# Turning the states' exponentials on TensorE instead of through DRAM, and VectorE's sums of the last batch placed later

## The chip, the cores and the metric

The kernel runs on one core of one Trainium2 chip. The metric is the device time of one execution in microseconds (us). Six executions of the kernel before gave a median of 720.07 us, from 718.45 to 720.99.

## The reference

`x` is (8, 8, 512, 64): 8 batches, 8 heads, 512 tokens of 64 values. `state` is (8, 8, 32, 64): 32 state tokens for each batch and head. Everything is float32.

```python
scores  = scale * x @ state^T;   a  = softmax(scores);   xread = a @ state     # 512 tokens
scores2 = scale * state @ x^T;   a2 = softmax(scores2);  sread = a2 @ x        # 32 state tokens
y = concat([xread, sread], axis=2) -> (8*544, 512)       # heads side by side
h = y @ w_in                                             # 512 -> 2048
out = (h * sigmoid(1.702 * h)) @ w_out                   # 2048 -> 512
```

## The kernel before

**How the work is cut.** Batch 0 and the up-projection of batch 1 run first, while the weights are still being rounded. Then comes one pass for each of the batches 1 to 7: `strassen_two(key, ...)` makes the down-projection of batch `key` as a Strassen product of seven partial products P1 to P7. In the passes 2 to 7, P5, P6, P3, P7 and P4 are themselves made as Strassen products of seven small products (`strassen_low`, matmuls in L693), so that P6.3 means "within P6, behind its third small product". Pass 1 (called *plain* in the code) does so for P6 and P7 alone. While pass `b` runs, the attention of batch `b + 1` is worked in at hooks such as "P5.6" or "P6", and the up-projection of a batch (`up_strassen`, L1091) runs at the head of its pass. After pass 7 the 256 state tokens of all batches ("sr") go through `up_strassen("sr", ...)` and `strassen("sr", ...)`, and the kernel ends with their four stores.

**What sets the order.** The order is written out by hand: each engine takes its instructions strictly in the order of the code, and a hook puts its work into the queues of all engines at that place. `hooks_next(b)` lists what is worked in for batch `b`. SyncE issues all DMAs, in order.

**The states' softmax.** `att_scores` leaves the scores of the 32 states of 4 heads in 128 partitions, one bank of 128x512 for each half `g` (0 or 1). `att_s_exp` makes the exponentials (`e2`, ScalarE, L372) and their sums, and `s_norm` the inverse of the sums (VectorE, two tiny operations for each half, L378 and L379). `att_sread` (TensorE, L500) needs the exponentials turned, tokens on the partitions, in the tile `eT`. For batches 0 and 1 `att_eT` does it (L489): four 128x128 transposes on TensorE for each half, and a ScalarE copy out of PSUM (L490). For batches 2 to 7 the turn goes through memory: `eT_out` writes the blocks to the DRAM tile `squares` in four DMAs (L468), `eT_in` fetches them back in four more (L476), and `eT_turn` finishes within 32x32 blocks by one VectorE transpose for each half (L480). The inverse sums are then applied to the small result of `att_sread` by two ScalarE operations (L509).

**The sums of a pass.** Each Strassen product needs sums of its operands, made by VectorE (`tt`, L751; on the weights `T_of`, L1235). `low_load` fetches sums of the weights that are kept in DRAM: `low_load(6, 1)` is issued behind P5 and read by P3's second small product, `low_load(3, 0)` is issued behind P6 and read by P7's second. P7's left operand S3 has four steps of sums, `steps3`, of two 128x256 additions each. They stand behind P3 and behind the hook "run". In the passes 2 to 6 that hook holds TensorE work (`att_sread`, `att_M`); in pass 7, which has no next batch, it holds only the issue of one load.

**The sums for the state tokens.** `sr_sums` lists 20 VectorE operations: 0 to 15 on halves of `w_in` (128x512 each, L1051), 16 to 19 on the state tokens (128x256). They are worked into pass 7, as are five operations `low_third` that put quarters of `w_out` back as they were (L1235).

**`strassen_low` and the banks.** Of its seven small products, the first and third write bank x, the second, fifth and seventh bank y, the fourth and sixth bank z. ScalarE copies x after the first product (L702) and after the third (L708), VectorE adds after the others (L698), and a product that writes a bank again waits until it was read. `up_strassen` works in the same way with `begin(u)`, `end(u - 1)` and `middle(u)` for u = 0 to 3; its additions are L1101, and `s12` and `s3` make sums for the product that follows.

Of the kernel before, what the change touches and what calls it, by code (L numbers as in the profile page):

```python
# [20 lines left out]
def kernel(  # L21
# [337 lines left out]
            nc.vector.tensor_scalar(mx, mx, scale, None, ALU.mult)  # L359
            a["mx2"].append(mx)  # L360

    e2_room = {}

    def att_s_exp(b, room=None):
        a = A[b]
        if room is None:
            room = e2_room[b] = apool.tile([P, NPR, S], FP32, tag="xT", name=f"e2_{b}")
        a["e2"] = []
        for g in range(NG):
            e = room[:, g]  # L370
            sm = apool.tile([P, 1], FP32, tag="sm2", name=f"sm2_{b}_{g}", bufs=4)
            nc.scalar.activation(out=e, in_=a["s"][g], func=AF.Exp, bias=a["mx2"][g], scale=scale, accum_out=sm)  # L372
            a["e2"].append((e, sm))

    def s_norm(b, g):

        e, sm = A[b]["e2"][g]
        nc.vector.tensor_scalar(sm, sm, eps, None, ALU.add)  # L378
        nc.vector.reciprocal(out=sm, in_=sm)  # L379
        if b < 2:  # L380
            nc.vector.tensor_scalar(e, e, sm, None, ALU.mult)

    def att_s_norm(b):
        for g in range(NG):
# [74 lines left out]
        for g in range(NG):  # L459
            nc.scalar.copy(m[:, g], ps[g])  # L460


    squares = dram.tile([Ns, NG * NB, NPR, Ns], FP32, name="squares")

    def eT_out(b):
        for j in range(NPR):
            src = e2_room[b][Ns * j : Ns * (j + 1), :NG].rearrange("n g (t a) -> n (g t) a", a=Ns)
            nc.sync.dma_start(squares[:, :, j], src)  # L468

    def eT_in(b):  # L470

        a = A[b]
        a["eT"] = apool.tile([P, NG, SCH, P], FP32, tag="eT", name=f"eT_{b}")
        v = squares.rearrange("n (k i) j a -> i n k (j a)", i=SCH)
        for i in range(SCH):
            nc.sync.dma_start(a["eT"][Ns * i : Ns * (i + 1)].rearrange("n g c q -> n (g c) q"), v[i])  # L476

    def eT_turn(b, g):
        t = A[b]["eT"][:, g].rearrange("p c q -> p (c q)")
        nc.vector.transpose(t, t)  # L480

    def att_eT(b, g):

        a = A[b]
# [7 lines left out]
    def att_sread(b):  # L492

        a = A[b]
        ps = att_ps([P, NG, D], f"sr_{b}")
        for g in range(NG):
            for c in range(SCH):
                for j in range(NPR):
                    st = slice(Ns * j, Ns * (j + 1))
                    nc.tensor.matmul(  # L500
                        ps[st, g], a["eT"][:, g, c, st], xn[b][:, c, NG * j + g],
                        start=(c == 0), stop=(c == SCH - 1),
                    )
        sr = apool.tile([P, P], FP32, tag="sr", name=f"sr_{b}")
        if b < 2:
            nc.scalar.copy(sr, ps.rearrange("p g d -> p (g d)"))
        else:
            for g in range(NG):
                nc.scalar.activation(out=sr[:, D * g : D * (g + 1)], in_=ps[:, g], func=AF.Copy, scale=a["e2"][g][1])  # L509
        A[b]["sr"] = sr  # L510

    def att_srT(b):
# [210 lines left out]
    def strassen_two(key, dst, hooks, a4):  # L723
# [10 lines left out]
        def hook(name):  # L734
            for fn, args in hooks.get(name, ()):
                fn(*args)
# [75 lines left out]
        if plain:  # L812
            for fn in first:
                fn()
            p5 = bank(0)
            product(p5, [S1[:, f, :half] for f in range(HF)], T1, "P5")
            hook("P5")
            banks = [h0, h1, o]
        else:

            def at(i):
                for fn in first[i - 1 : i]:
                    fn()
                hook(f"P5.{i}")

            b11, t3, b21, b22 = halves_of(T1)
            strassen_low(left_of(S1, *r), (b11, t3, b21, b22, *low_b), [h0, h1, o], p5, at)
            low_load(6, 1)
            hook("P5")
            o, h0, h1 = low_banks()  # L830
            banks = [h0, o, h1]

# [45 lines left out]
        if plain:  # L878
            for fn in steps3:
                fn()  # L880
            hook("P6")
            p3 = bank(3)
            product(p3, A_of(0, 1), B22, "P3")
            o, h0, h1 = low_banks()
            lowly("P7", left3, T3, low_b, [h0, h1, o], k3, {})
        else:
            hook("P6")
            p3 = o01
            o, h0, h1 = low_banks()
            lowly("P3", left12, B22, low_b, [h0, h1, o], p3, {1: steps12[2:3], 2: steps12[3:]})  # L890
            if key + 1 < B:
                low_load(5, 1)
            hook("run")
            for fn in steps3:
                fn()
            hook("T")
            o, h0, h1 = low_banks()
            lowly("P7", left3, T3, low_a, [o, h0, h1], k3, {k + 1: steps4[k : k + 1] for k in range(4)})
            if key + 1 < B:
                low_load(2, 0)  # L900
# [25 lines left out]
    def hooks_next(b):  # L926

        h = {}

        def at(name, fn, *args):  # L930
            h.setdefault(name, []).append((fn, args))

        at("P1a", att_state, b)
        at("P2a", att_scores, b)

        at("P2a", load_x, b)
        at("P2a", att_M, b, 0)
        at("P2a", att_M, b, 1, True)
        at("P2a", att_blocks, b)
        at("P2a", att_s_max, b)  # L940
        at("P2a", att_s_exp, b)
        at("P2a", eT_out, b)
        at("P2a", x_max, b, 0)
        at("P2a", x_sub, b, 0)
        if b > 2:
            at("P5.1", x_exp, b, 0)
            at("P5.6", att_s_norm, b)
            at("P5.6", x_max, b, 1)
            at("P5.7", x_sub, b, 1)
            at("P6.1", x_exp, b, 1)  # L950
        else:
            at("P2a", x_max, b, 1)
            at("P2a", x_sub, b, 1)
            at("P2a", x_exp, b)
            at("P2", att_s_norm, b)
        steps = up_sums(b)

        A[b]["sums"] = {0: steps[9:11], 1: [steps[11], steps[14]]}
        attention = [
            ("P6.1", x_sum, 0), ("P6.3", x_sum, 1), ("P6.3", x_inverse), ("P6.4", x_scale, 0),  # L960
        ]
        if b > 2:
            attention += [("P6.6", x_scale, 1), ("P3.3", x_back, 0), ("P3.4", x_back, 1), ("P3.5", eT_turn, 0), ("P3.6", eT_turn, 1)]
            names = {"T": range(5), "P7.5": (5, 6), "P7.6": (7,), "P4.1": (8,), "P4.5": (12, 13)}
            run, turned = "run", "P7.2"
        else:
            attention += [("P6.5", x_scale, 1), ("P6.6", x_back, 0), ("P6", x_back, 1), ("P6", eT_turn, 0), ("P6", eT_turn, 1)]
            names = {"P3a": range(7), "P7.1": (7,), "P7.2": (8,), "P7.3": (12, 13)}
            run, turned = "P3a", "P3b"
        attention += [("P5", eT_in), (run, att_sread), (run, att_M, 3, True), (run, att_M, 2)]  # L970
        for name, fn, *args in attention:
            at(name, fn, b, *args)
        for name, n in names.items():
            for i in n:
                at(name, steps[i][0], *steps[i][1])
        at(turned, att_srT, b)
        return h
# [92 lines left out]

        return steps, left, [each(v) for v in (r11, r21, r22, *ts)]

    def up_strassen(b, ntok, left, right, between=()):

        QT = ntok // 2
        b11, b21, b22, t1, t2, t3, t4 = right
        banks = {}
# [22 lines left out]
        def add(ps, x, dst):  # L1100
            nc.vector.tensor_tensor(out=dst, in0=ps, in1=x, op=ALU.add)  # L1101


        def begin(u):
            l11, l12, l21, l22, m1, m2, m4 = left(u)
# [2 lines left out]
            c21, _ = quarters(b, NU + u, ntok)  # L1108
            nc.scalar.copy(c21, product(u, "x", l11, b11, True))
            add(product(u, "y", m2, t2, True), c21, c12)  # L1110

        def middle(u):
            l11, l12, l21, l22, m1, m2, m4 = left(u)
# [4 lines left out]
            add(product(u, "y", l21, t3, False), c21, c22)  # L1118
            add(z, c22, c22)
            gelu(c22, c22)  # L1120

        def end(u):
            l11, l12, l21, l22, m1, m2, m4 = left(u)
# [3 lines left out]
            gelu(c21, c21)  # L1127
            add(product(u, "z", m4, b22, False), c12, c12)
            gelu(c12, c12)
            if u:  # L1130
                s12(b, u - 1, ntok)

# [141 lines left out]
    for b in range(1, B):  # L1274
# [18 lines left out]
        else:  # L1293

            steps, left, right = sr_sums()
            order = (
                ("P5.6", 2), ("P6.1", 3), ("P6.2", 6), ("P6.3", 7), ("P6.4", 8), ("P3.3", 9), ("P3.4", 10), ("P3.5", 11),
                ("P7.5", 12), ("P7.6", 13), ("P4.1", 16, 17), ("P4.5", 18, 19), ("P4.6", 14), ("P4.7", 15),
            )
            hooks = {name: [steps[i] for i in n] for name, *n in order}  # L1300
            hooks["P3.6"] = [(low_third, (T1,))]
            hooks["P4.7"] += [(low_third, (t,)) for t in (T2, T3, T4, B22)]
            ahead["P1a"][:0] = [steps[i] for i in (0, 1, 4, 5)]
        for name, first in ahead.items():
            hooks[name] = first + hooks.get(name, [])
# [9 lines left out]
    nb = P // Ns  # L1315
    strassen(
        "sr", B * Ns, lambda r, n: out_s[nb * r.start : nb * r.stop, :, n],
        [[(up_strassen("sr", B * Ns, left, right), ())]],
    )


# [28 lines left out]
```

## Time and profile before

| What | Before |
|---|---|
| median of 6 executions | 720.07 us |
| the profiled execution | 719.47 us, span 717.7 us |
| outside the span | 1.8 us |
| TensorE busy | 700.6 us, 98% of the span |
| VectorE busy | 591.4 us, 82% |
| ScalarE busy | 229.8 us, 32% |
| DMA | 74.73 MB, 135849 packets, 113008 of them under 512 B |

In the lists of instructions a line gives the start in us from the start of the span, the duration (for a merged group: first start to last end), engine, source line, operation, tiles (out<-in) and count, and in brackets how long the engine stood idle before and what it was waiting for. TensorE's matmuls are pipelined: the duration of one is longer than the distance between two starts, so the distance of starts is what a matmul costs in a row. A float32 matmul leaves two records, a transpose leaves one.

### The profile page before, as it was taken

To read this page: it belongs to the slowest core of one execution; us is meant where nothing else is said; L and a number is where in the kernel's file an instruction comes from. 1 tells how busy PE (TensorE), PEld (TensorE's weight loads), DVE (VectorE), ACT (ScalarE), POOL (GpSimd) and SP (SyncE) were. 2 spreads that over 40 slices of the span, in tenths; PEclk is the share of its full clock that TensorE was granted. 3 is DMA by queue.
4 is the path that set the end of the run, shared out by engine and by line. 5 is a ranking of instruction groups with operands and counts; after the bars stand their busy time and mean duration, and the time that the engine had idled before them with its cause. 6 is when DMAs were issued, how large, how long until landed. Compare 5 with 4: busy or idle time off the path is not lost.

```text
span 717.7 us, 12333 instructions
## 1 busy us (share of the span) xinstructions
PE 700.6 (98%) x4903; PEld 557.2 (78%) x4903; DVE 591.4 (82%) x1211; ACT 229.8 (32%) x449; POOL 0.8 (0%) x8
## 2 busy tenths in 40 slices
PE   8989999999899999999999999999999999999996
PEld 3433444467698799888998899879987998899995
DVE  6998899739967999789968997799789986989440
ACT  5686511023114322433233322441243125200210
POOL 0000000000000000000000000000000000000000
PEclk9999999999999999999999999999999999999999
DMA  9921246017344194407450564136432740031001
GB/s 233 359 89 55 92 148 149 2 59 165 93 164 83 34 179 157 92 1 161 150 145 5 108 196 131 26 74 176 160 52 49 172 162 16 1 121 56 16 1 30
DMA packets 135849, 74.73 MB, mean 104 GB/s; under 512 B 113008, under 2 KB 126832, under 8 KB 135792
## 3 DMA queue, kind: packets, MB, share of 16 engines
q1 hardware_dynamic: 135792, 73.94, 38.6%
q8 instruction: 39, 0.64, 0.4%
q14 instruction: 18, 0.15, 0.1%
HBM read 57.93 MB, written 15.99 MB: 103 GB/s over the span
## 4 chain that ended last, share of the span: by engine, by line
PE 85%; DVE 7%; DMA 4%; ACT 2%; issue 1%; SPq 0%; DVEq 0%; ACTq 0%
PE o L1091 17%; PE low L693 17%; PE o L744 13%; PE o L693 8%; PE o L542 7%; PE h L524 7%; PE upx L1091 6%; PE M L320 4%; PE o L585 2%; DVE later L751 1%; PE o L320 1%; PE sr L500 1%; DMA low<-low 1%; PE warm L125 1%; DVE g L751 1%; DMA out_dram<-osb_sr 1%
## 5 line engine op out<-in xcount | busy, mean ns | idle before, releaser
L1101 DVE TENSOR_TENSOR g<-o,g 128x512 f32<-128x512 f32 (+1 forms) x140 | 88.0, 650 | 55.5 <-PE o L1091 54.5
L744 PE MATMUL o<-w_out,g 128*128 128x256 f32 x480 | 107.9, 381 | 0.0
L744 PEld LDWEIGHTS o<-w_out,g 128*128 128x128 f32 x480 | 90.1, 190 | 18.4 <-issue 6.3
L1098 ACT ACTIVATE g<-g 128x512 f32<-128x512 f32 (+1 forms) x84 | 49.8, 600 | 101.9 <-DVE g L1101 101.9
L1091 PE MATMUL upx<-aT,M 128*128 128x256 f32 x192 | 49.3, 379 | 0.0
L1091 PE MATMUL o<-ta,M 128*128 128x256 f32 x192 | 49.3, 379 | 0.0
L1091 PE MATMUL o<-ta,ms 128*128 128x256 f32 x192 | 48.3, 379 | 0.0
L460 ACT COPY M<-M 128x512 f32<-128x512 f32 x64 | 33.2, 596 | 28.1 <-PE M L320 28.1
L1091 PEld LDWEIGHTS o<-ta,ms 128*128 128x128 f32 x192 | 36.5, 190 | 5.0
L1091 PEld LDWEIGHTS o<-ta,M 128*128 128x128 f32 x192 | 36.5, 190 | 5.0
L693 PE MATMUL low<-low,g 128*128 128x128 f32 x304 | 40.2, 275 | 0.0
L1091 PEld LDWEIGHTS upx<-aT,M 128*128 128x128 f32 x192 | 36.1, 190 | 4.7
L693 PEld LDWEIGHTS low<-low,g 128*128 128x128 f32 x304 | 37.0, 192 | 0.0
L693 PE MATMUL low<-sums,later 128*128 128x128 f32 x264 | 35.0, 275 | 0.1
L693 PEld LDWEIGHTS low<-sums,later 128*128 128x128 f32 x264 | 32.7, 192 | 0.7 <-DVE pu L698 0.3
L565 DVE TENSOR_TENSOR later<-g,g 128x512 f32<-128x512 f32 (+1 forms) x32 | 20.8, 650 | 15.0 <-ACT g L527 15.0
L320 PE MATMUL M<-w_in,stT 64*32 64x512 f32 x512 | 32.7, 594 | 0.2 <-ACT eT L490 0.2
L524 PE MATMUL h<-low,M 128*128 128x512 f32 x64 | 29.8, 600 | 1.5 <-DVE low L408 1.5
L524 PE MATMUL h<-aT,M 128*128 128x512 f32 x64 | 28.7, 599 | 1.4 <-ACT M L460 1.4
L542 PE MATMUL o<-w_out,g 128*128 128x512 f32 x64 | 28.7, 594 | 0.0
L693 PE MATMUL low<-w_out,g 128*128 128x128 f32 x216 | 28.5, 275 | 0.0
L542 PE MATMUL o<-w_out,sums 128*128 128x512 f32 x64 | 28.4, 594 | 0.0
(215 smaller groups left out, 1271.5 us busy)
## 6 DMA issues: line engine op xcount, KB each, us to landing
low<-low SPq DMA_DIRECT2D x34, 768.0 KB
later<-in_moe_w_out_dram SPq DMA_DIRECT2D x16, 512.0 KB
xn<-in_x_dram SPq DMA_DIRECT2D x28, 256.0 KB
w_out<-in_moe_w_in_dram SPq DMA_DIRECT2D x12, 512.0 KB
xsq<-in_x_dram SPq DMA_DIRECT2D x96, 64.0 KB
out_dram<-osb SPq DMA_DIRECT2D x18, 256.0 KB
out_dram<-later SPq DMA_DIRECT2D x14, 256.0 KB
squares<-e SPq DMA_DIRECT2D x24, 128.0 KB
```

What stands on the lines that cost most here:

```text
L320: nc.tensor.matmul(ps[g][st], A[b]["stT"][rows, st], rhs(rows, j), start=True, stop=True)
L460: nc.scalar.copy(m[:, g], ps[g])
L524: nc.tensor.matmul(hps, lhs[i], rhs[i], start=(i == 0), stop=(i == n - 1))
L542: nc.tensor.matmul(ops, G[key, f // 2][:, f % 2, P * r : P * (r + 1)], w_out[:, f], start=(f == 0), stop=(f == NF - 1))
L565: nc.vector.tensor_tensor(out=s1, in0=a21, in1=a22, op=ALU.add)
L585: nc.tensor.matmul(ps[:, r], lhs[f][:, P * r : P * (r + 1)], rhs[:, f], start=(first and r == 0 and f == 0), stop=(f == HF - 1), skip_grou ...
L693: nc.tensor.matmul(ps, lhs[f], rhs[:, f], start=(first and f == 0), stop=(f == QF - 1), skip_group_check=True)
L744: nc.tensor.matmul(ps[:, r], lhs[f][:, P * r : P * (r + 1)], rhs[:, f], start=(r == 0 and f == 0), stop=(f == HF - 1), skip_group_check=True,)
L751: nc.vector.tensor_tensor(out=out, in0=x0, in1=x1, op=op)
L1091: nc.tensor.matmul(ps[:, k], lhs[i][:, o : o + P], rhs[i], start=(first and k == 0 and i == 0), stop=(i == n - 1), skip_group_check=True,)
L1098: nc.scalar.activation(out=dst, in_=src, func=AF.Gelu_apprx_sigmoid)
L1101: nc.vector.tensor_tensor(out=dst, in0=ps, in1=x, op=ALU.add)
```

## The change

It does three things.

1. For batches 2 to 7, `eT_out`, `eT_in`, `eT_turn` and the DRAM tile are gone. `s_norm` now scales the exponentials themselves, on ScalarE, at its old place, and `att_eT` (four transposes on TensorE and one ScalarE copy for each half) stands in the hook "P6", between P6 and P3. One plain ScalarE copy takes `att_sread`'s result. In the passes 2 to 6 `x_scale(1)`, `x_back(0)` and `x_back(1)` stand one hook later or in the places that `eT_turn` left.
2. In pass 7 the four steps of `steps3` stand behind P3's third to sixth small product, not behind P3.
3. In pass 7 ten of VectorE's operations for the state tokens (`sr_sums` 10 to 15 and four `low_third`) stand in `up_strassen("sr", ...)`, one behind the additions of each `begin`, `middle` and `end` (there ahead of `s12`), until they are used up; `aside()` places them. `sr_sums` 6 to 9 and one `low_third` move to later hooks.

```diff
     def s_norm(b, g):
...
         if b < 2:
             nc.vector.tensor_scalar(e, e, sm, None, ALU.mult)
+        else:
+            nc.scalar.activation(out=e, in_=e, func=AF.Copy, scale=sm)
-    squares = dram.tile([Ns, NG * NB, NPR, Ns], FP32, name="squares")
-    def eT_out(b):
...
-    def eT_in(b):
...
-    def eT_turn(b, g):
...
     def att_sread(b):
...
-        if b < 2:
-            nc.scalar.copy(sr, ps.rearrange("p g d -> p (g d)"))
-        else:
-            for g in range(NG):
-                nc.scalar.activation(out=sr[:, D * g : D * (g + 1)], in_=ps[:, g], func=AF.Copy, scale=a["e2"][g][1])
+        nc.scalar.copy(sr, ps.rearrange("p g d -> p (g d)"))
...
-            lowly("P3", left12, B22, low_b, [h0, h1, o], p3, {1: steps12[2:3], 2: steps12[3:]})
+            own3 = {1: steps12[2:3], 2: steps12[3:]}
+            if key + 1 == B:
+                own3.update({i + 3: steps3[i : i + 1] for i in range(4)})
+            lowly("P3", left12, B22, low_b, [h0, h1, o], p3, own3)
...
             hook("run")
-            for fn in steps3:
-                fn()
+            if key + 1 < B:
+                for fn in steps3:
+                    fn()
...
-            ("P6.1", x_sum, 0), ("P6.3", x_sum, 1), ("P6.3", x_inverse), ("P6.4", x_scale, 0),
+            ("P6.1", x_sum, 0), ("P6.3", x_sum, 1), ("P6.3", x_inverse), ("P6.4", x_scale, 0), ("P6", att_eT, 0), ("P6", att_eT, 1),
         if b > 2:
-            attention += [("P6.6", x_scale, 1), ("P3.3", x_back, 0), ("P3.4", x_back, 1), ("P3.5", eT_turn, 0), ("P3.6", eT_turn, 1)]
+            attention += [("P3.3", x_scale, 1), ("P3.4", x_back, 0), ("P3.5", x_back, 1)]
         else:
-            attention += [("P6.5", x_scale, 1), ("P6.6", x_back, 0), ("P6", x_back, 1), ("P6", eT_turn, 0), ("P6", eT_turn, 1)]
+            attention += [("P6.5", x_scale, 1), ("P6.6", x_back, 0), ("P6", x_back, 1)]
...
-    def up_strassen(b, ntok, left, right, between=()):
+    def up_strassen(b, ntok, left, right, between=(), beside=()):
...
+        def aside():
+            if beside:
+                fn, args = beside.pop(0)
+                fn(*args)
...
-                ("P5.6", 2), ("P6.1", 3), ("P6.2", 6), ("P6.3", 7), ("P6.4", 8), ("P3.3", 9), ("P3.4", 10), ("P3.5", 11),
-                ("P7.5", 12), ("P7.6", 13), ("P4.1", 16, 17), ("P4.5", 18, 19), ("P4.6", 14), ("P4.7", 15),
+                ("P5.6", 2), ("P6.1", 3), ("P6.3", 6), ("P6.4", 7), ("P7.5", 8), ("P7.6", 9), ("P4.1", 16, 17), ("P4.5", 18, 19),
-            hooks["P3.6"] = [(low_third, (T1,))]
-            hooks["P4.7"] += [(low_third, (t,)) for t in (T2, T3, T4, B22)]
+            hooks["P3.7"] = [(low_third, (T1,))]
+            beside = steps[10:16] + [(low_third, (t,)) for t in (T2, T3, T4, B22)]
```

More of the change, by code (lines that the diff above doesn't have):

```diff
@@ L360, in att_s_max @@
             a["mx2"].append(mx)
-    e2_room = {}
     def att_s_exp(b, room=None):
@@ L366, in att_s_exp @@
         if room is None:
-            room = e2_room[b] = apool.tile([P, NPR, S], FP32, tag="xT", name=f"e2_{b}")
+            room = apool.tile([P, NPR, S], FP32, tag="xT", name=f"e2_{b}")
         a["e2"] = []
@@ L460, in att_M @@
             nc.scalar.copy(m[:, g], ps[g])
-    squares = dram.tile([Ns, NG * NB, NPR, Ns], FP32, name="squares")
-    def eT_out(b):
-        for j in range(NPR):
-            src = e2_room[b][Ns * j : Ns * (j + 1), :NG].rearrange("n g (t a) -> n (g t) a", a=Ns)
-            nc.sync.dma_start(squares[:, :, j], src)
-    def eT_in(b):
[L472 to L476, printed above, removed]
-    def eT_turn(b, g):
-        t = A[b]["eT"][:, g].rearrange("p c q -> p (c q)")
-        nc.vector.transpose(t, t)
     def att_eT(b, g):
@@ L816, in strassen_two @@
             product(p5, [S1[:, f, :half] for f in range(HF)], T1, "P5")
-            hook("P5")
             banks = [h0, h1, o]
@@ L828, in strassen_two @@
             low_load(6, 1)
-            hook("P5")
             o, h0, h1 = low_banks()
@@ L941, in hooks_next @@
         at("P2a", att_s_exp, b)
-        at("P2a", eT_out, b)
         at("P2a", x_max, b, 0)
@@ L966, in hooks_next @@
         else:
-            attention += [("P6.5", x_scale, 1), ("P6.6", x_back, 0), ("P6", x_back, 1), ("P6", eT_turn, 0), ("P6", eT_turn, 1)]
+            attention += [("P6.5", x_scale, 1), ("P6.6", x_back, 0), ("P6", x_back, 1)]
             names = {"P3a": range(7), "P7.1": (7,), "P7.2": (8,), "P7.3": (12, 13)}
             run, turned = "P3a", "P3b"
-        attention += [("P5", eT_in), (run, att_sread), (run, att_M, 3, True), (run, att_M, 2)]
+        attention += [(run, att_sread), (run, att_M, 3, True), (run, att_M, 2)]
         for name, fn, *args in attention:
@@ L1071, in sr_sums @@
         return steps, left, [each(v) for v in (r11, r21, r22, *ts)]
-    def up_strassen(b, ntok, left, right, between=()):
+    def up_strassen(b, ntok, left, right, between=(), beside=()):
+        beside = list(beside)
         QT = ntok // 2
@@ L1110, in begin @@
             add(product(u, "y", m2, t2, True), c21, c12)
+            aside()
         def middle(u):
@@ L1120, in middle @@
             gelu(c22, c22)
+            aside()
         def end(u):
@@ L1129, in end @@
             gelu(c12, c12)
+            aside()
             if u:
@@ L1317 @@
         "sr", B * Ns, lambda r, n: out_s[nb * r.start : nb * r.stop, :, n],
-        [[(up_strassen("sr", B * Ns, left, right), ())]],
+        [[(up_strassen("sr", B * Ns, left, right, beside=beside), ())]],
     )
```

## The prediction

> **What bounds the kernel now.** I read the page first: busy times and the chain that ended last.
>
> ```profile
> PE 700.6 (98%) x4903; PEld 557.2 (78%) x4903; DVE 591.4 (82%) x1211; ACT 229.8 (32%) x449; POOL 0.8 (0%) x8
> PE 85%; DVE 7%; DMA 4%; ACT 2%; issue 1%; SPq 0%; DVEq 0%; ACTq 0%
> ```
>
> TensorE is busy for 98% of the span and carries 85% of the chain. So an instruction added to TensorE costs its full slot, one taken from VectorE, ScalarE or a DMA gains nothing by itself, and the only gain to be had is a wait of TensorE that goes away. The second view is therefore the list of TensorE's waits, the third its instructions in order of time around each of them.
>
> ```profile
> PE sr L500 <- DVE eT L480: 2.3, 1, 2.3
> PE o L1091 <- DVE g L1101: 0.8, 1, 0.8
> PE low L693 <- DMA low<-low: 0.7, 1, 0.7
> PE low L693 <- ACT pu L702: 0.5, 1, 0.5
> PE low L693 <- DVE later L698: 0.2, 1, 0.2
> ```
>
> These are all the waits that the change comes near; the rest lie in the first 95 us or are tails of these. They must be priced by distances of starts, since the idle time is counted from a modelled end.
>
> **Added: the transposes.** Twelve halves of four, 48 in all. Batch 0 already turns its exponentials in this way:
>
> ```profile
> 81.34 1.04 PE L489 MATMUL eT<-ident,e 128*128 128x128 f32 x8
> 82.62 1.58 PE L320 MATMUL M<-w_in,stT 64*32 64x512 f32 x16 [0.24 <-ACT eT L490]
> ```
>
> Eight take 1.04 with the last one's 0.27, so seven distances fill 0.77: 0.11 each, 0.88 for a batch, 48 x 0.11 = **5.28 us**. The pause after these eight (0.24 idle) is the next matmul's wait for a PSUM buffer that the copy must empty. In the new place P3 follows, in other banks, so I take no pause; if it stays, six times 0.24 + 0.17 (the usual overlap of a start with the end before it) = 2.5 us more. That is the upper bound, 7.7; the lower is 5.28, since no row shows a shorter distance.
>
> The Trainium skill speaks against the change here: "TensorE: Matmul & The Clock Gate", Part 4: PE-mode transpose, gives about 275 ns for a transpose in a kernel and says that transposes do not count as activity for the clock. By that figure 48 would cost an estimated 13.2 us and the kernel would lose about 7 us. The trace has the same 272 ns as duration of one, but starts 0.11 apart, and the page's row of granted clock shows 9 in every slice, those with batch 0's and 1's turns included; so I reckon with the distance.
>
> The copies of the turned halves on ScalarE (12 x 0.59, L490's mean) and the scalings (12 x 0.63, L1098's mean on 128x512 in SBUF) add 15 us to an engine that is 32% busy. What is queued behind them matters. The scalings come at P5.6; behind them stands P6's copy of bank x, and P6's third product waits for that.
>
> ```profile
> 562.41 0.16 DVE L379 RECIPROCAL sm<-sm 128x1 f32<-128x1 f32 x1
> 563.60 0.27 ACT L702 COPY pu<-low 128x128 f32<-128x128 f32 x1 [4.25 <-PE low L693]
> 564.25 1.06 PE L693 MATMUL low<-sums,later 128*128 128x128 f32 x8
> ```
>
> The first reciprocal ends at 562.32, two scalings end by 563.6, the copy keeps its 563.60, and it has 0.38 to spare before 564.25. ScalarE sat idle for 4.25 ahead of it: cost nothing. The copies run beside P3's first product (0.89), whose own copy of x comes after it: nothing. `att_sread` reads `eT` a whole P3 later.
>
> **Removed: DMAs and VectorE's turns.** 48 DMAs of 128 KB, and 12 transposes of 0.69 (8.2 us, L480). Both lie beside TensorE, except where TensorE waits for them:
>
> - Pass 1. P3's first half has sixteen records of 0.216 from 185.60, 3.45, and 0.10 for the change of tile, as in pass 6 (574.34 + 0.89 + 0.10 = 575.33). The next matmul could start at 189.15.
>
> ```profile
> 190.84 1.26 DVE L480 STREAM_TRANSPOSE eT<-eT 128x512 f32<-128x512 f32 x2
> 191.56 1.25 PE L500 MATMUL sr<-xn,eT 128*32 128x64 f32 x64 [2.34 <-DVE eT L480]
> ```
>
>   It starts 2.41 late, and its 64 records take 1.18 to the next group, against 1.03 in pass 6: 2.56 in all. In the changed kernel `eT` comes from TensorE and ScalarE ahead of P3, so the whole 2.56 goes. VectorE is next in line: its queue ends with `x_back(1)` at 190.9, while `att_sread`, pushed back by the 0.88, would run from 190.0 to 191.1; the sums behind it overwrite what it reads, so they start with it, 1.6 earlier than now, and no product waits for them before P7. **-2.56.**
> - Pass 2. P3's second product waits for `low_load(6, 1)`:
>
> ```profile
> 265.03 1.06 PE L693 MATMUL low<-w_out,g 128*128 128x128 f32 x8
> 266.82 1.13 PE L693 MATMUL low<-low,spare_M 128*128 128x128 f32 x8 [0.74 <-DMA low<-low]
> 272.35 1.43 PE L500 MATMUL sr<-xn,eT 128*32 128x64 f32 x64
> ```
>
>   1.79 between the starts instead of 0.89, and 0.97 instead of 0.89 for the product itself: 0.98. The transposes stand ahead of P3, so the product asks 0.88 later for a load that is issued as before, and `eT_in`'s four DMAs no longer run beside it: **-0.98**. `att_sread` takes 1.36 to the next group instead of 1.03, as its second half waits for the second turn: **-0.33**.
> - Pass 6: 568.76 to 569.80, then 0.97, the same load: **-0.23**. Passes 3 to 5 show no such wait, so their transposes are a plain loss.
>
> VectorE loses two operations per pass between P6.6 and P3.6, and gets none; `x_back(1)` still ends ahead of the sums that read its result.
>
> **Moved: `steps3` and the ten operations in pass 7.**
>
> ```profile
> 647.85 1.06 PE L693 MATMUL o<-w_out,g 128*128 128x128 f32 x8
> 649.45 1.13 PE L693 MATMUL low<-low,later 128*128 128x128 f32 x8 [0.54 <-ACT pu L702]
> 652.20 1.06 PE L693 MATMUL low<-w_out,g 128*128 128x128 f32 x8
> 653.49 1.16 PE L693 MATMUL low<-w_out,later 128*128 128x128 f32 x8 [0.23 <-DVE later L698]
> 664.31 1.06 PE L1091 MATMUL upx_sr<-srT,w_in 128*128 128x128 f32 x8
> 666.12 1.16 PE L1091 MATMUL o<-ta_sr,w_in 128*128 128x128 f32 x8 [0.75 <-DVE g L1101]
> ```
>
> P7's second product starts 1.60 after the first, not 0.89, and then takes 0.97: 0.79. It needs S3's second step, which VectorE makes at 648.93 (the copy named in the brackets had no part in it). Its sixth waits for an addition in the same backlog: 1.29 and 0.99, so 0.50. In `up_strassen` the third product on bank y waits for an addition that stands behind two L1051 and four L1235: 1.81 and 0.99, so 1.02. Sum 2.31.
>
> In P3 the four steps (0.67 a pair) take the places of three L1051 and one L1235 (0.60 each), so P3's last additions come up to 0.3 later. P3's sixth product already waits 0.05 for one; I book 0.1. In `up_strassen("sr")` one u has five additions, two sums of `s12` (0.42 each) and now three operations of 0.68: 2.9 + 2.0 = 4.9, against seven products of 0.89 = 6.2 on TensorE. The least slack is in `middle`: the addition on y ends 0.42 after it may start, and bank y is asked for again 1.5 after that. So no new wait: **-2.31 + 0.1 = -2.2.** The operations stand ahead of the `begin`, `middle` or `end` that reads them.
>
> **The sum.** 5.28 - 2.56 - 0.98 - 0.33 - 0.23 - 2.2 = **-1.0 us**. The profiled execution goes from 719.47 to 718.4 (span 716.7). It lies 0.6 below the median of the six, so the median goes from 720.07 to 719.0. The bound of what a measurement of this kernel can tell is 0.2%, 1.4 us: 718.6 to 721.5 is "no change".
>
> **Rivals.**
>
> - *The forecast as it stands, 719.0 (0.56).*
> - *The waits move on (0.20).* VectorE is 97% busy from 160 to 192 (31.07 of 32 us) and stays so in P3 of pass 7. If P7 still waits there, 1.3 of the 2.31 is not gained, and if P7 of pass 1 meets VectorE's backlog, up to 0.9 of the 2.56: -1.0 + 1.3 + 0.9 = +1.2, 721.3, or half of that. Against it: VectorE is idle for 2.52 ahead of P7's second addition at 200.34, and pass 7's 3.0 us of sums leave the place where they were waited for.
> - *Slower: the scalings hold up P6's copy of x (0.07).* ScalarE is strictly in order. From the point where the reciprocals come over 0.4 late, or a scaling takes over 0.8 (the dearest 128x512 row of ScalarE is 0.72, L219), P6's third product waits; with one scaling exposed in the passes 2 to 6, 5 x 0.63 = 3.2: -1.0 + 3.2 = +2.2, 722.2. The times at 562 speak against it.
> - *More than forecast (0.17).* Two more waits in pass 1 (its P6, 182 to 184, 0.39 and 0.45 by starts) are VectorE's backlog, and passes 3 to 6 have a late addition of 0.07 each in P3. If the lighter VectorE takes these too: -1.0 - 0.84 - 0.28 = -2.1, 717.9. Nothing that stands ahead of P6 in pass 1 is taken from VectorE, which speaks against the larger part.
> - *The turn was not needed as assumed* cannot be: the order of TensorE's queue shows exactly twelve more groups of four transposes and no other difference.
>
> **The numbers.** The sum of -1.0 lies only 0.4 from the bound of "faster", and the terms are read to 0.1 each, some twelve of them; so of the forecast's own 0.56 I give 0.14 to faster. Faster 0.14 + 0.16 = 0.30; slower 0.07, and 0.01 of the moved waits: 0.08; same 0.62. The range goes from the lighter-VectorE case with some spread, 717.6, to the middle of the moved waits, 720.8.
>
> **What would show it.** Right: 64 L489-like transposes in all (16 before), the new ones in six groups of eight with starts 0.11 apart and P3's first product 0.11 after the last; `att_sread` 0.10 after P3 in every pass, pass 1 included; the wait for `low` gone; in pass 7 no gap over 0.1 from P3 to the state tokens' P1; TensorE's busy time up by about 5, its idle time down by about 6. Wrong: a gap of TensorE on either side of the transposes, ScalarE's L702 later than P6's first product, or the pass from 329 to 405 longer by anything but 0.9.

## The result and the profile after

| | before | after |
|---|---|---|
| median | 720.29 us (718.42 to 722.07, 50 executions) | 718.10 us (717.99 to 718.38, 23 executions) |
| profiled execution | 719.47 us, span 717.7 | 718.08 us, span 716.3 |

The ratio of the times is 0.9973, 95% interval 0.9966 to 0.998: faster by 0.27%. The profiled executions differ by 1.4 us, the medians by 2.2, and the executions of the changed kernel lie within 0.4 us of each other where those of the kernel before ranged over 3.7. The second and third of these were not forecast.

The page's busy times and chain, and of the list of TensorE's waits the two longest rows and the only one behind 100 us:

```profile
PE 703.1 (98%) x4951; PEld 560.8 (78%) x4951; DVE 586.8 (82%) x1199; ACT 241.7 (34%) x467; POOL 0.8 (0%) x8
PE 90%; DVE 3%; DMA 3%; ACT 2%; issue 0%; SPq 0%; DVEq 0%; ACTq 0%
...
PE h L500 <- DVE low L408: 1.5, 1, 1.5
PE h L500 <- ACT M L460: 1.4, 2, 0.8
PE o L669 <- DVE later L674: 0.2, 1, 0.2
```

TensorE's share of the chain rose from 85% to 90%, VectorE's fell from 7% to 3%. The waits of `att_sread` for `eT`, of P3 for the load of `low` and of `up_strassen` for VectorE's additions are no longer in the list; its longest are those of the first 95 us. TensorE's instructions in order of time at the places of the prediction (L469 is the transpose, L480 `att_sread`, L669 the small products, L720 P3 of pass 1, L1071 `up_strassen`):

```profile
185.60 1.04 PE L469 MATMUL eT<-ident,e 128*128 128x128 f32 x8
186.47 3.62 PE L720 MATMUL o<-w_out,g 128*128 128x256 f32 x16
190.02 1.10 PE L480 MATMUL sr<-xn,eT 128*32 128x64 f32 x64
...
569.11 1.04 PE L469 MATMUL eT<-ident,e 128*128 128x128 f32 x8
569.98 1.06 PE L669 MATMUL low<-w_out,g 128*128 128x128 f32 x8
...
648.81 1.06 PE L669 MATMUL o<-w_out,g 128*128 128x128 f32 x8
649.71 1.06 PE L669 MATMUL low<-low,later 128*128 128x128 f32 x8
652.39 1.06 PE L669 MATMUL low<-w_out,g 128*128 128x128 f32 x8
653.28 1.06 PE L669 MATMUL low<-w_out,later 128*128 128x128 f32 x8
664.00 1.06 PE L1071 MATMUL upx_sr<-srT,w_in 128*128 128x128 f32 x8
664.89 1.06 PE L1071 MATMUL o<-ta_sr,w_in 128*128 128x128 f32 x8
```

The eight transposes of a batch take 0.87 from their start to P3's in pass 1 and in pass 6; there is no gap on either side. In the part of pass 7 shown here all distances of products are 0.89 or 0.90. All terms of the forecast stand side by side further down.

### The profile page after: what moved, and what is told of

It reads as the page before. It is cut to its first block, busy times and chain, and to the rows that moved or that the text cites. A ratio compares the mean times of both kernels' runs of the same rounds, so it can differ in the third digit from the quotient of the medians.

```text
span 716.3 us, 12331 instructions
## 1 busy us (share of the span) xinstructions
PE 703.1 (98%) x4951; PEld 560.8 (78%) x4951; DVE 586.8 (82%) x1199; ACT 241.7 (34%) x467; POOL 0.8 (0%) x8
## 4 chain that ended last, share of the span: by engine, by line
PE 90%; DVE 3%; DMA 3%; ACT 2%; issue 0%; SPq 0%; DVEq 0%; ACTq 0%
PE low L669 19%; PE o L1071 17%; PE o L720 14%; PE o L669 9%; PE o L518 7%; PE h L500 7%; PE upx L1071 6%; PE M L320 4%; PE o L561 2%; PE o L320 1%; PE sr L480 1%; PE warm L125 1%; PE upx_sr L1071 1%; DMA out_dram<-osb_sr 1%; PE eT L469 1%; DMA out_dram<-osb 1%
## 5 line engine op out<-in xcount | busy, mean ns | idle before, releaser
L720 PE MATMUL o<-w_out,g 128*128 128x256 f32 x480 | 107.9, 381 | 0.0
L720 PEld LDWEIGHTS o<-w_out,g 128*128 128x128 f32 x480 | 90.1, 190 | 18.4 <-issue 6.3
L1071 PE MATMUL upx<-aT,M 128*128 128x256 f32 x192 | 49.3, 379 | 0.0
L1071 PE MATMUL o<-ta,M 128*128 128x256 f32 x192 | 49.3, 379 | 0.0
L1071 PE MATMUL o<-ta,ms 128*128 128x256 f32 x192 | 48.3, 379 | 0.0
L1071 PEld LDWEIGHTS o<-ta,ms 128*128 128x128 f32 x192 | 36.5, 190 | 5.0
L1071 PEld LDWEIGHTS o<-ta,M 128*128 128x128 f32 x192 | 36.5, 190 | 5.0
L669 PE MATMUL low<-low,g 128*128 128x128 f32 x304 | 40.2, 275 | 0.0
L1071 PEld LDWEIGHTS upx<-aT,M 128*128 128x128 f32 x192 | 36.1, 190 | 4.7
L669 PEld LDWEIGHTS low<-low,g 128*128 128x128 f32 x304 | 37.0, 192 | 0.0
L669 PE MATMUL low<-sums,later 128*128 128x128 f32 x264 | 35.0, 276 | 0.1
L669 PEld LDWEIGHTS low<-sums,later 128*128 128x128 f32 x264 | 32.7, 192 | 0.7 <-DVE pu L674 0.3
L669 PE MATMUL low<-w_out,g 128*128 128x128 f32 x216 | 28.5, 275 | 0.0
```

Of the source, the lines that this page charges most:

```text
L669: nc.tensor.matmul(ps, lhs[f], rhs[:, f], start=(first and f == 0), stop=(f == QF - 1), skip_group_check=True)
L720: nc.tensor.matmul(ps[:, r], lhs[f][:, P * r : P * (r + 1)], rhs[:, f], start=(r == 0 and f == 0), stop=(f == HF - 1), skip_group_check=True,)
L1071: nc.tensor.matmul(ps[:, k], lhs[i][:, o : o + P], rhs[i], start=(first and k == 0 and i == 0), stop=(i == n - 1), skip_group_check=True,)
```

## The experiments

The first question was why the medians differ by more than the profiles, and why the spread went. Theory A: the DMAs of the turn make `low_load(6, 1)` late by an amount that varies. Rival B: the spread is at the start or the end of the kernel.

**Two more profiles of the kernel before.** No edit.

> The kernel before, unchanged, for a second profile. Its executions range over 3.6 us, those of the changed kernel over 0.4. Theory A (the traffic of the turn through DRAM makes the load of weight sums late by an amount that varies): without TensorE's waits for the tile low the first profile would be 719.47 - 0.98 - 0.23 = 718.3, and the time of this execution is 718.3 plus its own waits of P3's second product in the passes 2 to 6, all other waits of TensorE the same within 0.1. Rival B (the start or the stores at the end vary): the waits for low are 1.2 as before, and the difference lies before 160 us or behind 700 us.

> As the second profile of the kernel before. Theory A: 718.3 plus the waits of P3's second product for low; rival B: the difference lies at the start or the end.

Measured: 721.13 and 721.92 us, spans 719.3 and 720.1. Both theories fell. The waits for `low` did move: by the distances of starts, in pass 2 0.19 instead of 0.98 in one and 0.6 in the other, in pass 3 0.9 to 1.0 in both where the first profile had none, in pass 6 nothing in one and 0.6 in the other. Their sums are 1.1 and 2.2, so theory A has 719.4 and 720.5 for these executions, 1.7 and 1.4 too little. Nearly all of that rest is in pass 1, right behind TensorE's wait for `eT`: from the start of `sr` to P3's second half the second and third execution take 1.5 and 1.6 more than the first (in the second, another 0.2 lies in the first 10 us). These rows are the stretches 192 to 194 and 194 to 196 us, of the first profile and of the second; the columns are stretch, length, busy time and count of TensorE, its weight loads, VectorE, ScalarE and GpSimd, then the granted clock, DMA share and GB/s.

```profile
192.00:194.00 2.00, 2.00 (x72) 1.13 (x68) 1.19 (x3) 0.60 (x3) 0.00 (x0) 1.00 0.03 8
194.00:196.00 2.00, 2.00 (x22) 1.25 (x7) 1.97 (x5) 1.97 (x4) 0.00 (x0) 1.00 0.11 43
```

```profile
192.00:194.00 2.00, 2.00 (x69) 1.30 (x66) 0.80 (x2) 0.52 (x2) 0.00 (x0) 0.56 0.00 0
194.00:196.00 2.00, 2.00 (x32) 0.44 (x16) 1.93 (x5) 0.61 (x3) 0.00 (x0) 0.58 0.03 8
```

The granted clock is 1.00 in the first and 0.56 and 0.58 in the second. (1 - 0.56) x 2 + (1 - 0.58) x 2 = 1.72 us at full clock are lost, as much as 3.4 us at half speed cost. TensorE's list shows where they go (the second profile of before):

```profile
191.74 1.67 PE L500 MATMUL sr<-xn,eT 128*32 128x64 f32 x64 [2.34 <-DVE eT L480]
193.35 3.06 PE L320 MATMUL M<-w_in,stT 64*32 64x512 f32 x32
```

`sr` takes 1.67 where the first profile had 1.25, and `M` 3.06 where it had 1.95. The third profile has the same (clock 0.53 and 0.62). So the profile on which I built was one execution in which the clock stayed full behind the pause; 1.6 us more are lost where it does not.

**Part 1 alone.** Against the changed kernel the sums go back, and so do the hooks of `sr_sums` and `low_third`, with nothing in `beside`.

```diff
-            if key + 1 == B:
-                own3.update({i + 3: steps3[i : i + 1] for i in range(4)})
...
-            if key + 1 < B:
-                for fn in steps3:
-                    fn()
+            for fn in steps3:
+                fn()
```

> Part 1 alone: the turn on TensorE, with VectorE's sums of the last batch where they were. By the sum of the prediction the moved sums are worth 2.3, so 718.1 + 2.3 = 720.4, span 718.6. Theory A: the executions lie within 0.6 of each other, since the DMAs are gone. Rival B: they range over 3 us or more, as the kernel before does.

Measured: 720.41 us (720.33 to 721.31, 12 executions), span 718.6; ratio 0.9998, interval 0.9989 to 1.0007. Median and span came as expected. Nine executions lie within 0.21 us, three at 720.7 to 721.3, so the spread is mostly gone, though not quite as far as expected. By the medians, the turn on TensorE by itself is worth nothing that can be measured. That is the sum of two things: against the first profile of before, where the clock stayed full, the span is 0.9 longer (718.6 against 717.7), against the second and third 0.7 and 1.5 shorter.

**Parts 2 and 3 alone.** The diff of parts 2 and 3 on the kernel before, nothing of part 1.

> Parts 2 and 3 alone: the sums of the last batch moved, the turn still through DRAM. The last pass gains 2.3 in every execution: median 720.3 - 2.3 = 718.0. Theory A: its executions still range over 3 us (716.1 to 719.8). Rival B, if the spread came from the end of the kernel: under 1 us.

Measured: 717.68 us (717.06 to 718.56, 6 executions); ratio 0.9956, interval 0.994 to 0.9971. The median is 0.3 under the expected one and 0.4 under the changed kernel's. The spread of 1.5 lies between the two expectations and decides nothing. The distance to the 720.71 of the kernel before beside it, 3.0, is more than the 2.3 that the moved sums are worth. The mean granted clock of the executions fits that: it is 0.997 in two of these six executions (717.74 and 718.56) and higher in the others, and 0.997 or less in 15 of the 17 of the kernel before. The profiled one has full clock behind the pause.

**The pause of pass 1 filled.** After those profiles I had a new theory, A2: behind the pause of 2.4 us the clock drops to half in most executions.

```diff
+    def fill_gap(b):
+        ps = att_ps([P, FC], "gap")
+        for _ in range(2):
+            nc.tensor.matmul(ps, w_in[0][:, 0, :P], w_in[0][:, 1], start=True, stop=True)
...
+        if b == 2:
+            attention += [(run, fill_gap)]
```

> The kernel before with two matmuls of weights, read by nobody, in TensorE's pause of 2.4 us in pass 1 (1.7 of it filled, 0.7 left); nothing else changes. Theory A2 (the pause makes the clock drop to half for 3.4 us in most executions, worth 1.7, in two of three profiles): the clock stays full, and the executions end at 718.3 plus the waits for low (0.6 to 1.8): median 719.4, range 718.8 to 720.1, 1 us under the kernel before. Rival B2 (the spread lies in the DMAs alone): median and range as before, 720.3 to 720.7.

Measured: 719.01 us (718.54 to 719.56, 10 executions); ratio 0.998, interval 0.9971 to 0.9989. TensorE's list now has the wait for `eT` at 0.6, and the stretches have full clock:

```profile
PE sr L500 <- DVE eT L480: 0.6, 1, 0.6
```

```profile
192.00:194.00 2.00, 2.00 (x72) 1.14 (x68) 1.19 (x3) 0.60 (x3) 0.00 (x0) 1.00 0.04 8
194.00:196.00 2.00, 2.00 (x22) 1.25 (x7) 1.97 (x5) 1.98 (x4) 0.00 (x0) 1.00 0.10 40
```

A2 holds: two matmuls that nobody reads make the kernel before 1.6 us faster by the medians (720.62 beside it), and the range shrinks from 3.2 to 1.0. The Trainium skill, "TensorE: Matmul & The Clock Gate", Part 1, tells that the clock falls to half after an idle window of about 3.4 us that runs freely of the program. The length of the slow stretch agrees (3.4 us by the rows). The pause does not: 2.4 us were enough, which that section's rule of no gaps over some 3.4 us would let pass; here the measurement decides.

The window can be seen in the three profiles of the kernel before, whose traces say when the granted clock changes. It is full from 6.71 us on in the first, 4.52 in the second and 4.39 in the third, and each later change lies a whole number of windows of 3.413 us behind that: the two falls in pass 1 55 windows (192.25 and 192.12), the two returns 56. Counted on in this way, a border of two windows at 191.03 splits the first profile's pause, and in the other two profiles the pause lies wholly within one window. First the two windows beside that border in the first profile, then the window with the pause and the next one in the second:

```profile
187.61:191.03 3.42, 1.61 (x8) 1.08 (x6) 3.42 (x11) 0.00 (x0) 0.00 (x0) 1.00 0.00 0
191.03:194.44 3.41, 2.88 (x96) 1.57 (x96) 2.57 (x5) 1.04 (x4) 0.00 (x0) 1.00 0.02 5
```

```profile
188.84:192.25 3.41, 1.07 (x35) 0.66 (x33) 3.41 (x8) 0.00 (x0) 0.00 (x0) 1.00 0.00 0
192.25:195.66 3.41, 3.41 (x68) 1.51 (x64) 2.14 (x5) 0.78 (x3) 0.00 (x0) 0.50 0.02 5
```

In the second profile, and likewise in the third, a window with 1.07 us of TensorE's work was followed by one at half clock; in the first, windows with 1.61 and 2.88 were not. So in these profiles it was the place of the pause among the windows that decided. How often the clock falls shows in the mean clock of each execution, which 3.4 us at half clock lower by 0.0024: of the 20 executions of the kernel before beside this run, the five with 0.998 or 0.999 took 718.60 to 719.93, the fifteen with 0.995 to 0.997 took 720.24 to 721.84. All ten with the pause filled have 0.998 or 0.999.

**Part 2 undone in the changed kernel.**

```diff
-            if key + 1 == B:
-                own3.update({i + 3: steps3[i : i + 1] for i in range(4)})
...
-            if key + 1 < B:
-                for fn in steps3:
-                    fn()
+            for fn in steps3:
+                fn()
```

> The changed kernel with part 2 undone: S3's sums of pass 7 behind P3 again. By the prediction's terms P7's second and sixth product wait again, 0.79 + 0.50: 718.1 + 1.3 = 719.4. If part 3 alone had emptied VectorE's queue: 718.1.

Measured: 719.91 us (719.84 to 720.00, 10 executions), 1.8 over the changed kernel, not 1.3. VectorE's and TensorE's lists show the surplus:

```profile
649.12 0.68 DVE L1219 TENSOR_TENSOR sums<-sums 128x512 f32<-128x512 f32 x1
649.72 0.75 DVE L727 TENSOR_TENSOR later<-g,g 128x256 f32<-128x256 f32 x2
650.91 1.13 PE L669 MATMUL low<-low,later 128*128 128x128 f32 x8 [1.14 <-ACT pu L678]
```

The `low_third` that part 3 moved to P3.7 now stands between P3's last addition and `steps3` and makes P7's second product 0.6 later again. Both waits are back (1.37 and 0.50 by starts), so part 2 and part 3 are not independent terms.

**The turn on TensorE only where TensorE waited.** If the passes 2 to 6 pay 0.87 each for the transposes and get back only waits, the better kernel keeps the way through DRAM there. Against the kernel before, batch 2 is turned on TensorE, batches 3 to 7 as before, and parts 2 and 3 are taken over.

```diff
         if b < 2:
             nc.vector.tensor_scalar(e, e, sm, None, ALU.mult)
+        elif b < 3:
+            nc.scalar.activation(out=e, in_=e, func=AF.Copy, scale=sm)
...
+        if b < 3:
+            attention += [("P6", att_eT, 0), ("P6", att_eT, 1)]
```

> The turn on TensorE for batch 2 alone (pass 1, where TensorE waited), through DRAM for batches 3 to 7, and parts 2 and 3. Against parts 2 and 3 alone with a full clock (span 716.1) pass 1 gains 2.56 - 0.88 = 1.68: span 714.4, time 716.2, with a range of 1 us from the waits for low. Theory: faster than the changed kernel by 1.9, since the five turns of the passes 2 to 6 cost it 5 x 0.88 and give back only the waits. Rival (the turn through DRAM costs more elsewhere than these waits): 718.1 or more.

Measured: 715.80 us (715.19 to 716.03, 5 executions); ratio 0.9932, interval 0.9919 to 0.9944. As expected, 2.3 under the changed kernel.

**The same with `eT_in` held back.**

```diff
+    def eT_gate(b):
+        a = A[b]
+        a["eT"] = apool.tile([P, NG, SCH, P], FP32, tag="eT", name=f"eT_{b}")
+        nc.vector.memset(a["eT"][:, 0, 0, :1], 0.0)
...
-            attention += [("P5", eT_in)]
+            attention += [("P6.2", eT_gate), ("P6.2", eT_in)]
```

> As the one before, and eT_in is made to start 1.5 to 2 us later, behind a one-column memset of its tile at P6.2, so that it does not run beside the load of low that P3 waits for. Theory A (eT_in's traffic delays that load): no wait for low in P3, 1 us less: span 713.3, time 715.1, range under 0.6, as long as the turned halves still land before P3.5. Rival (the load is late by the blocks written before, or by itself): waits as without the memset, 716.2.

Measured: 714.76 us (714.52 to 715.05, 5 executions); ratio 0.9918, interval 0.9905 to 0.9932: faster than both kernels. P3's first two products of pass 2, without and with the memset:

```profile
263.50 1.06 PE L695 MATMUL low<-w_out,g 128*128 128x128 f32 x8
265.65 1.13 PE L695 MATMUL low<-low,spare_M 128*128 128x128 f32 x8 [1.09 <-DMA low<-low]
```

```profile
263.45 1.06 PE L699 MATMUL low<-w_out,g 128*128 128x128 f32 x8
264.34 1.06 PE L699 MATMUL low<-low,spare_M 128*128 128x128 f32 x8
```

The distance falls from 2.15 to 0.89. Apart from the small memset on VectorE only the start of `eT_in` was moved, from 1.0 to 2.9 us behind the issue of the load, so its four DMAs of 128 KB are what made the load of 768 KB late in pass 2. Theory A did not come out whole, though: in pass 6 a wait is left, 0.5 by the distances of starts. The list puts it down to VectorE, but the product also waits for the load, which lands at 567.58, 0.14 ahead of its start; in the first profile, pass 2, it is 0.13.

The traces say when each of these loads landed. From issue to landing, in the passes 2 to 6:

| Profile | DMAs of the turn | us to landing |
|---|---|---|
| changed kernel | none | 4.1 to 4.4 |
| kernel before, three profiles | 0.5 to 1.2 us behind the load | 5.0 to 7.8 |
| batch 2 alone turned on TensorE | 0.6 to 1.0 us behind the load | 8.1 in pass 2, 5.2 to 6.2 in the others |
| the same, `eT_in` held back | 2.9 us behind the load | 7.3 in pass 6, 4.1 to 5.4 in the others |

With `eT_in` close behind it the load lands later in every pass, and TensorE waits where it takes 7 us or more. In which passes it does differs from profile to profile: parts 2 and 3 alone, with the same DMAs, had no such wait in pass 2 and waits of 1.1 and 0.9 in the passes 3 and 6. One profile of each kernel would therefore not be enough; the times of the five executions with the memset and of the five without do not overlap.

## Why the prediction was right, and where it was not

The forecast was 719.0 with a range of 717.6 to 720.8; 718.10 lies in it, on the side to which I had given 0.30. By its own steps:

| Term | forecast | measured between the two first profiles |
|---|---|---|
| 48 transposes | +5.28 | +5.24 (0.87 a batch) |
| pass 1, wait for `eT` | -2.56 | -2.56 |
| pass 2, wait for `low` | -0.98 | -0.97 |
| pass 2, half of `att_sread` | -0.33 | -0.33 |
| pass 6, wait for `low` | -0.23 | -0.22 |
| pass 7, three waits | -2.31 | -2.29 |
| pass 7, P3's late additions | +0.1 | -0.04 |
| passes 3 to 5, P3's sixth product | 0 | -0.20 |
| pass 6, scalings ahead of P6 | 0 | +0.03 |
| sum | -1.0 | -1.3 (the spans: -1.4) |

- *The transposes.* The distance of starts, 0.11, was the right price. The page's 275 ns, an estimate of 13.2 us in the prediction, did not come: 48 took 5.2, and the granted clock is 1.00 where they run. The row of granted clock on the profile's page was no ground to reckon with that, as the prediction did: a slice of it is 18 us long, 3.4 us at half clock leave 0.9 of it, and the second profile of before has the same forty nines in that row.
- *The scalings on ScalarE* were sized too cheaply. I let the first one start with the first reciprocal, at 562.3, let both end 1.28 later, and gave the copy of x 0.38 to spare. In order of time, ScalarE in pass 6 after, and TensorE's third product of P6:

```profile
563.00 1.33 ACT L381 ACTIVATE e<-e,sm 128x512 f32<-128x512 f32 x2 [3.34 <-DVE sm L377]
564.25 0.24 ACT L678 COPY pu<-low 128x128 f32<-128x128 f32 x1
564.56 1.14 PE L669 MATMUL low<-sums,later 128*128 128x128 f32 x8
```

  The two take 1.33, close to that, but the first starts late: here 0.37 after the first reciprocal's end, 0.1 after the second's; in the passes 2 to 5 it starts 0.1 after the first's, and why pass 6 differs no run shows. The copy comes 0.4 behind the end of P6's first product (0.1 before), which the prediction had named as a sign of being wrong, and the third product lost 0.08, in this pass alone. The slower rival was that close.
- *The lighter VectorE.* The small half of the fourth rival came true (0.07 each in the passes 3 to 5), the larger did not, as argued: P6 of pass 1 still waits 0.39 and 0.45.
- *The step that failed* is the last of the sum: "It lies 0.6 below the median of the six, so the median goes from 720.07 to 719.0." The offset was carried over as if it belonged to the kernel. It belonged to an execution with a full clock in pass 1. Most executions before held, beside the terms above, about 1.6 us lost at half clock, and some held longer waits for `low` (2.2 in the third profile, 1.2 in the first); the change takes these too. That the measured median still lay in the range is owed to its width, which was made for other rivals. The profile's own forecast, 718.4, was the better number for the median: it missed by 0.3, by the rows of P3's additions in the table.
- *The signs.* TensorE's busy time was to rise by about 5 and its idle time to fall by about 6; they moved by 2.5 and 3.9. A price by distances of starts takes in time that the profile counts as busy (pass 7's three waits are 2.29 by starts and 1.52 idle), and the profile after has a wait of 0.9 at 7.3 us, for the load of the states, which the first profile of before lacks and the other two have.
- *The chances* rested on the six executions shown, 718.45 to 720.99. I read their range as the noise of the measurement; it was a property of this kernel, and a range of 2.5 us in a kernel bound by one engine should have been asked for a cause.
- *What the change is worth* divides otherwise than its size suggests. The turn alone: nothing by the medians (0.9998), a loss of 0.9 in span against an execution with full clock. The moved sums alone: 0.9956, of which 2.3 us are the sums' and the rest goes with the clock. The five turns of the passes 2 to 6 cost 4.4 on TensorE and gave back 1.7 in the first profile's terms, and without them stand the two fastest kernels here.

What stays open: how little work a window of 3.413 us may hold before the clock falls (the limit lies between 1.07 and 1.61 us by these profiles), why the clock fell so seldom with parts 2 and 3 alone, and what made the load late in pass 6 with `eT_in` held back; there the rival, the blocks written before, is not excluded.

## What to carry to other kernels

On an engine that is 98% busy, price every step by the distance of starts, and price a stall the same way: the six large terms came out within 0.1 each. Ask of a kernel whose executions spread why they do before taking one profile for all of them; a second profile showed here in one row what the first could not. Where a step has two implementations, on the bounding engine and beside it, choose for each place: the bounding engine only where it was waiting anyway.

## What the runs showed of the hardware that was not expected

- A pause of TensorE of 2.4 us was followed by 3.413 us at half clock in two of three profiles (192.25 to 195.66 in the second), and filling 1.7 us of the pause with matmuls that nobody reads kept the clock at 1.00.
- In these two profiles the clock fell and rose at whole windows of 3.413 us (55 and 56) from where it first was full; in the profile in which a border of two windows split the pause, it did not fall.
- A load of 768 KB landed 4.1 to 4.4 us after its issue when nothing was issued behind it for 6 us, and 5.0 to 7.8 when four DMAs of 128 KB were issued on the same queue 0.5 to 1.2 us behind it; 2.9 us behind it, 4.1 to 5.4 in four passes and 7.3 in one.
- Of two scalings on ScalarE, each with its own reciprocal from VectorE, the first began 0.1 us behind the end of the first reciprocal in the passes 2 to 5, but in pass 6 only at 563.00, 0.1 behind the second, though the first was ready at 562.63.
